# One time to landing for transfers of all sizes, in the planner that orders the instructions of an attention and mixer kernel

## The chip, the cores and the metric

The kernel runs on one core of a Trainium2 chip. The metric is device time in microseconds (us) of one execution. Five engines work from instruction streams of their own, each in order: PE (matmuls and transposes), ACT, DVE and POOL (elementwise work), and SP, which here issues every DMA.

## The reference, cut to what matters

All data are float32. Attention over 4 batches, 12 heads, 448 tokens, head size 64, with RMS-normalised q and k; then a gated block with a spatial matrix over the tokens; then a token mixer and a channel mixer with a residual.

```python
q_n, k_n = rmsnorm(q, g_q), rmsnorm(k, g_k)
attn = softmax(q_n @ k_n.T / 8);  x = attn @ v            # 48 heads, then (4, 448, 768)
h = relu(x @ w_in);  u, v = h[..., :512], h[..., 512:]    # w_in 768x1024
v_s = w_spatial @ layernorm(v) + b_spatial                # over the tokens
x = (u * v_s) @ w_out                                     # w_out 512x768
u = x + (relu(x.T @ w_tok1) @ w_tok2).T                   # 448 -> 256 -> 448
out = u + relu(u @ w_ch1) @ w_ch2                         # 768 -> 1536 -> 768
```

## The kernel before, in words

The work is recorded first and ordered afterwards. Every call on `nc` makes an `Op` with an engine, a cost, and a time `late` that passes after its end until its result can be seen elsewhere. `Plan.issue` (L365) then places all ops: a greedy list schedule (`place`, L263) runs over all engines at once, each engine taking, of the ops that are ready by the plan's own clock, the one with the least weight. It is run forward, the weights are taken from a run backward, and so on for eight rounds; the forward run with the shortest planned span is kept, and the ops are issued in its order of start times. So each engine's stream, SP's queue and the choice of PSUM banks all come from `estimate` (L214). What it returns never delays anything on the chip: there each engine takes its stream in order and waits on semaphores. An op that the plan holds ready and the chip does not, stops all that stands behind it on its engine.

For a transfer `estimate` gives two numbers (L244, L245): the time that SP is taken, the size over 260 bytes per ns and at least 475 ns, and the time to landing after that. `hop` (L257) adds `late` to the end of an op for whoever waits for it, SP itself included.

The stages are these.

- Attention, 24 pairs of heads. A pair's q and k come by six DMAs into a tile `raw` (two buffers): two `raw<-in_q`, then `raw<-in_k` in parts of 112x4x64, 64x64, 112x3x64 and 48x64. ACT squares them (`sq`), DVE sums (`ss`), POOL works out the root with two ACT calls `ry` and scales `raw` in place; PE transposes (`tp`), ACT evicts (`whole` for the first eight pairs, `qt` and `kt` later). Then scores `sc`, maxima `nm` on DVE, exponentials `e` on ACT with sums, transposes of `e` (`tp`), evictions `et`, products with v (`av`), results `xp`.
- Beside it the weights are prepared, float64 words turned to pairs of float32r: `word` and `wv` for w_in's second half (512 KB loads), `wpart` for all other weights in pieces (256 KB loads and two 128 KB stores to scratch each). ACT, DVE and POOL all take part.
- The gated block of a batch (`vps`, `ups`, `sps`, `xps`) can start when six pairs of the batch are done; the first three batches run beside the attention. It loads prepared weights (`wu` 768 KB, `wo` 1 MB) from scratch and stores `xo` to `x_d`.
- The last gated block runs beside the token mixer's start (`h1ps`, `u_ps`), then the channel mixer (`h2ps`, `o_ps`) runs to the end.

Of the kernel before, what the change touches and what calls it, by code (L numbers as in the profile page):

```python
# [149 lines left out]
class Plan:  # L150
# [63 lines left out]
    def estimate(self, engine, fn, out, ins, kwargs):  # L214

        shape = max((tuple(x.shape) for x in [out] + ins if isinstance(x, Part)), key=free)
        n = free(shape)
        psum = any(x.tile.psum for x in ins)
        if engine == "tensor":
            if fn == "transpose":  # L220
                return ins[0].shape[0] / 1.2 + 3, 200
            n = free(ins[1].shape)
            if ins[1].dtype == F32R:
                return 0.326 * n if ins[0].shape[0] <= 64 else n / 2.4 + 13, 200
            if ins[0].shape[0] <= 64:
                return 1.04 * n, 200
            return n / 1.2 + 54 if out.shape[0] <= 64 else n / 0.6, 200
        if engine == "scalar":
            extra = any(isinstance(kwargs.get(k), Part) for k in ("bias", "scale"))
            extra += kwargs.get("accum_out") is not None  # L230
            return 0.833 * n + (51 if psum else 94) + 93 * extra, 142
        if engine == "vector":
            if n <= 64:
                return 160, 128
            if fn in ("tensor_scalar", "tensor_copy") and not psum:
                return 0.53 * n + 90, 128
            pointer = fn == "scalar_tensor_tensor" and any(free(x.shape) == 1 for x in ins)
            return 1.042 * n + 70 + 61 * pointer, 175 if free(out.shape) < n else 128
        if engine == "gpsimd":
            if fn == "tensor_scalar":  # L240
                return max(165, 1.3 * n + 35), 75
            pace = 2.0 if any(x.steps and x.steps[-1][0] == "to_broadcast" for x in ins) else 2.4
            return max(165, pace * n + 20), 75
        size = shape[0] * n * 4  # L244
        return max(475, size / 260), 2400 + 1.2e-3 * size  # L245

    def fence(self, pools, act):

# [173 lines left out]
def free(shape):  # L422
    n = 1
    for x in shape[1:]:
        n *= x
    return n
# [905 lines left out]
```

## Time and profile before

| | |
|---|---|
| median of 3 runs | 947.33 us (947.18 to 949.82) |
| the profiled execution | 946.97 us |
| its span | 944.7 us |
| PE busy | 912.2 us (97%) |
| weight loads (PEld) busy | 738.3 us (78%) |
| DVE, ACT, POOL busy | 574.9, 454.1, 342.9 us |

PE is TensorE's matmuls, and a transpose counts as a matmul; DMA issue is not counted as busy. Rows name a group as output<-input. Source lines of the recorded ops are all that of the helper that issues them (L406), so one goes by tile names. Busy shares are averages over stages with different limits: attention alone at the start, gated blocks and attention mixed, then matmuls alone.

### The profile page before, as it was taken

To read this page: it belongs to the slowest core of one execution; us is meant where nothing else is said; L and a number is where in the kernel's file an instruction comes from. 1 tells how busy PE (TensorE), PEld (TensorE's weight loads), DVE (VectorE), ACT (ScalarE), POOL (GpSimd) and SP (SyncE) were. 2 spreads that over 40 slices of the span, in tenths; PEclk is the share of its full clock that TensorE was granted. 3 is DMA by queue.
4 is the path that set the end of the run, shared out by engine and by line. 5 is a ranking of instruction groups with operands and counts; after the bars stand their busy time and mean duration, and the time that the engine had idled before them with its cause. 6 is when DMAs were issued, how large, how long until landed. Compare 5 with 4: busy or idle time off the path is not lost.

```text
span 944.7 us, 15517 instructions
## 1 busy us (share of the span) xinstructions
PE 912.2 (97%) x5368; PEld 738.3 (78%) x5368; DVE 574.9 (61%) x1234; ACT 454.1 (48%) x1145; POOL 342.9 (36%) x478
## 2 busy tenths in 40 slices
PE   3888999999999999999999999999999999999998
PEld 1444465777767776677899999899899999999898
DVE  3988888765886767853151367635655546565434
ACT  4998978776686766764342344311312212122100
POOL 3565454784667744565044023100201102011100
PEclk9999999999999999999999999999999999999999
DMA  6555655457445465222764384721211112111024
GB/s 168 145 132 155 172 154 157 134 166 202 115 110 162 143 195 170 76 79 98 244 196 156 119 277 156 272 75 34 84 51 50 52 34 83 51 51 51 17 87 147
DMA packets 124653, 118.57 MB, mean 126 GB/s; under 512 B 74784, under 2 KB 108128, under 8 KB 123040
## 3 DMA queue, kind: packets, MB, share of 16 engines
q1 hardware_dynamic: 124576, 117.59, 41.3%
q8 instruction: 42, 0.69, 0.3%
q14 instruction: 35, 0.29, 0.1%
HBM read 89.77 MB, written 27.79 MB: 124 GB/s over the span
## 4 chain that ended last, share of the span: by engine, by line
PE 81%; ACT 8%; DMA 4%; DVE 2%; SPq 1%; issue 1%; POOL 1%; ACTq 0%; POOLq 0%
PE o_ps L406 19%; PE h2ps L406 18%; PE tp L406 8%; PE av L406 6%; PE xps L406 6%; PE vps L406 5%; PE sc L406 5%; PE ups L406 5%; PE sps L406 4%; ACT e L406 3%; PE u_ps L406 3%; PE h1ps L406 3%; SPq L406 1%; ACT et L406 1%; DMA x_d<-xo 1%
## 5 line engine op out<-in xcount | busy, mean ns | idle before, releaser
L406 PE MATMUL o_ps<-c,h 128*128 128x384 f32 x1008 | 179.9, 337 | 0.0
L406 PE MATMUL h2ps<-ut,c 128*128 128x512 f32 (+1 forms) x864 | 179.4, 364 | 0.0
L406 PEld LDWEIGHTS o_ps<-c,h 128*128 128x128 f32 x1008 | 175.0, 188 | 2.1 <-DVE acc L406 0.5
L406 PEld LDWEIGHTS h2ps<-ut,c 128*128 128x128 f32 x864 | 148.0, 189 | 24.1
L406 POOL TENSOR_TENSOR c<-word,c 128x384 fp32r<-128x384 f32 x40 | 40.5, 1014 | 271.8 <-ACT c L406 252.2
L406 ACT ACTIVATE e<-sc,nm 112x448 f32<-112x448 f32 x192 | 120.9, 639 | 31.6 <-PE tp L406 16.9
L406 DVE TENSOR_REDUCE nm<-sc 112x1 f32<-112x448 f32 x192 | 110.4, 615 | 25.1 <-PE sc L406 24.9
L406 PE MATMUL tp<-ident,e 112*128 112x112 f32 x672 | 96.7, 263 | 3.7 <-ACT et L406 1.3
L406 PEld LDWEIGHTS tp<-ident,e 112*128 112x128 f32 x672 | 73.5, 140 | 32.6 <-ACT et L406 7.4
L406 DVE TENSOR_TENSOR acc<-o_ps,acc 128x384 f32<-128x384 f32 x140 | 77.4, 556 | 29.5 <-PE o_ps L406 28.9
L406 POOL TENSOR_SCALAR e<-e,sums 112x448 f32<-112x448 f32 x112 | 71.2, 652 | 35.8 <-DVE sums L406 9.0
L406 ACT ACTIVATE c<-word 128x384 fp32r<-128x384 f32 x40 | 21.0, 525 | 128.3 <-DVE word L406 63.6
L406 ACT ACTIVATE h<-h2ps 128x512 fp32r<-128x512 f32 (+1 forms) x48 | 25.9, 539 | 111.7 <-PE h2ps L406 111.4
L406 DVE SCALAR_TENSOR_TENSOR h<-h2ps,h 128x512 fp32r<-128x512 f32 (+1 forms) x48 | 30.0, 624 | 80.8 <-ACT h L406 80.7
L406 ACT ACTIVATE et<-tp 128x448 f32<-128x448 f32 x120 | 65.1, 551 | 16.2 <-PE tp L406 13.8
L406 PE MATMUL ups<-xp,wu 128*128 128x448 f32 x288 | 69.9, 378 | 0.0
L406 PE MATMUL av<-et,v 128*64 128x448 f32 x288 | 66.7, 559 | 0.8 <-ACT et L406 0.5
L406 PE MATMUL xps<-wo,g 128*128 128x256 f32 x432 | 62.7, 291 | 0.4 <-ACT xo L406 0.4
L406 PEld LDWEIGHTS xps<-wo,g 128*128 128x128 f32 x432 | 54.9, 190 | 5.1 <-issue 2.0
L406 PEld LDWEIGHTS ups<-xp,wu 128*128 128x128 f32 x288 | 51.7, 188 | 6.8 <-ACT e L406 1.4
L406 DVE TENSOR_SCALAR word<-word 128x384 f32<-128x384 f32 (+1 forms) x92 | 35.1, 382 | 35.8 <-ACT word L406 34.3
L406 PE MATMUL vps<-wv,xp 128*128 128x512 f32 x216 | 56.0, 403 | 0.0
(112 smaller groups left out, 1460.0 us busy)
## 6 DMA issues: line engine op xcount, KB each, us to landing
raw<-in_moe_w_ch_dram SPq DMA_DIRECT2D x40, 384.0 KB, 3.2
wu<-wu_d SPq DMA_DIRECT2D x16, 768.0 KB, 4.7
wo<-wo_d SPq DMA_DIRECT2D x12, 1024.0 KB, 5.0
raw<-in_q_dram SPq DMA_DIRECT2D x48, 112.0 KB, 2.7
acc<-u_d SPq DMA_DIRECT2D x14, 384.0 KB, 8.2
out_dram<-o SPq DMA_DIRECT2D x28, 192.0 KB, 1.9
v<-in_v_dram SPq DMA_DIRECT2D x48, 96.0 KB, 2.6
x_d<-xo SPq DMA_DIRECT2D x36, 128.0 KB, 2.4
```

The costliest lines, as they stand in the source:

```text
L406: getattr(getattr(self.nc, op.engine), fn)(*args, **kwargs)
```

## The change

`estimate` returned for a transfer a landing time of 2400 ns plus 1.2 ns for every 1000 bytes; it returns 2000 ns for every size. The time that SP is taken stays as it was.

```diff
@@ -241,8 +241,7 @@
                 return max(165, 1.3 * n + 35), 75
             pace = 2.0 if any(x.steps and x.steps[-1][0] == "to_broadcast" for x in ins) else 2.4
             return max(165, pace * n + 20), 75
-        size = shape[0] * n * 4
-        return max(475, size / 260), 2400 + 1.2e-3 * size
+        return max(475, shape[0] * n * 4 / 260), 2000
```

No instruction is added or removed. The plan is another one on all engines, since a small shift of one start time moves all later choices; in the channel mixer the two orders are the same but for the last blocks. The file is one line shorter, so the same helper is L405 in the rows after.

SP's queue where the first two pairs have been asked for; `v_221` and `v_154` are the v tile of pair 0 under two numbers. Before:

```order
L406 DMA g<-in_g_k_dram 64x1
L406 DMA raw<-in_moe_w_in_dram 128x1024 x3
L406 DMA raw<-in_q_dram 112x4x64 x2
L406 DMA raw<-in_k_dram 112x4x64
L406 DMA raw<-in_k_dram 64x64
L406 DMA raw<-in_k_dram 112x3x64
L406 DMA raw<-in_k_dram 48x64
L406 DMA raw<-in_moe_w_in_dram 128x2x256
L406 DMA v_221<-in_v_dram 128x3x64 x2
```

The same place of SP's queue now:

```order
L405 DMA g<-in_g_k_dram 64x1
L405 DMA raw<-in_moe_w_in_dram 128x1024 x2
L405 DMA v_154<-in_v_dram 128x3x64 x2
L405 DMA vrest<-in_v_dram 64x64
L405 DMA raw<-in_q_dram 112x4x64 x2
L405 DMA raw<-in_k_dram 112x4x64
L405 DMA raw<-in_k_dram 64x64
L405 DMA raw<-in_k_dram 48x64
L405 DMA raw<-in_k_dram 112x3x64
L405 DMA vrest<-in_v_dram 64x64
L405 DMA raw<-in_moe_w_in_dram 128x1024
```

Pair 0's v stands ahead of pair 2's q and k, the third 512 KB load of w_in behind them, and the larger of a pair's last two k parts comes last instead of last but one (it does so for nearly all pairs).

ACT's stream at the same time, where pair 0's transposes are evicted (`whole`) and pair 1's root is begun (`ry`); `raw_128` is the first 512 KB of w_in. Before:

```order
L406 ACTIVATE sq_149<-raw_113 112x512
L406 ACTIVATE word_164<-raw_128 128x512
L406 ACTIVATE whole_169<-tp_154 128x448
L406 ACTIVATE whole_172<-tp_162,gg_144 128x448
L406 ACTIVATE ry_177<-ra_159 112x16
L406 ACTIVATE ry_177<-ry_177 112x16
```

And now:

```order
L405 ACTIVATE sq_149<-raw_113 112x512
L405 ACTIVATE word_152<-raw_128 128x512
L405 ACTIVATE ry_167<-ra_161 112x16
L405 ACTIVATE whole_172<-tp_156 128x448
L405 ACTIVATE whole_177<-tp_165,gg_143 128x448
L405 ACTIVATE ry_167<-ry_167 112x16
```

The first `ry` of pair 1 has moved ahead of pair 0's evictions; `word` still stands ahead of all of them.

SP's queue in the second gated block, where `xo` goes to `x_d` and a later pair's q and k are asked for. Before:

```order
L406 DMA x_d_67<-xo 128x256 x3
L406 DMA raw<-in_q_dram 112x4x64 x2
L406 DMA raw<-in_k_dram 112x4x64
L406 DMA wo<-wo_d_65 128x2048
L406 DMA x_d_66<-xo 64x256
L406 DMA x_d_67<-xo 64x256
L406 DMA raw<-in_k_dram 64x64
```

And now:

```order
L405 DMA x_d_67<-xo 128x256 x2
L405 DMA wo<-wo_d_65 128x2048
L405 DMA x_d_66<-xo 64x256
L405 DMA x_d_67<-xo 64x256
L405 DMA raw<-in_q_dram 112x4x64 x2
L405 DMA raw<-in_k_dram 112x4x64
L405 DMA x_d_67<-xo 128x256
L405 DMA raw<-in_k_dram 64x64
```

The two small stores of `xo` stand ahead of the pair's loads instead of among them.

## Rows read from the trace of the kernel before

**Rows 1.** The page: the span, and each engine's busy time.
```profile
span 944.7 us, 15517 instructions
PE 912.2 (97%) x5368; PEld 738.3 (78%) x5368; DVE 574.9 (61%) x1234; ACT 454.1 (48%) x1145; POOL 342.9 (36%) x478
```

**Rows 2.** Busy time by stretch: from:to length, engines with counts, PEclk, DMA share, GB/s.
```profile
core 0: us, PE busy (x) PEld busy (x) DVE busy (x) ACT busy (x) POOL busy (x), PEclk, DMA share, GB/s
0.00:25.00 25.00, 8.81 (x32) 4.01 (x32) 10.80 (x21) 13.09 (x30) 8.67 (x21) 1.00 0.64 160
25.00:116.70 91.70, 81.29 (x489) 40.64 (x489) 78.45 (x174) 84.59 (x235) 53.90 (x76) 1.00 0.55 154
116.70:460.00 343.30, 341.32 (x2179) 246.20 (x2178) 236.73 (x548) 237.21 (x645) 199.77 (x309) 1.00 0.49 142
460.00:930.00 470.00, 469.56 (x2607) 436.59 (x2605) 242.91 (x482) 118.87 (x236) 80.55 (x72) 1.00 0.33 105
930.00:944.70 14.70, 11.20 (x70) 10.88 (x68) 6.00 (x11) 0.38 (x1) 0.00 (x0) 1.00 0.41 148
```

**Rows 3.** Waits of PE, 0 to 130 us: total us, times, longest.
```profile
PE sc L406 <- ACT e L406: 4.0, 6, 1.1
```

**Rows 4.** Timeline of ACT, 9 to 17.5 us: start, us, instruction, idle before it.
```profile
14.91 0.66 ACT L406 ACTIVATE word<-raw 128x512 f32<-128x512 f32 x1 [2.03 <-DMA raw<-in_moe_w_in_dram]
15.47 0.54 ACT L406 ACTIVATE whole<-tp 128x448 f32<-128x448 f32 x1
16.42 0.22 ACT L406 ACTIVATE ry<-ra 112x16 f32<-112x16 f32 x1
```

**Rows 5.** Timeline of PE, 10 to 24 us.
```profile
10.86 1.75 PE L406 MATMUL tp<-ident,raw 112*128 112x112 f32 x8 [10.86 <-POOL raw L406]
16.59 5.00 PE L406 MATMUL sc<-whole 64*112 64x448 f32 x12 [3.97 <-ACT whole L406]
```

**Rows 6.** Timeline of SP, 9 to 14 us.
```profile
9.68 1.53 SPq L406 DMA_DIRECT2D raw<-in_moe_w_in_dram  x3
12.78 1.05 SPq L406 DMA_DIRECT2D raw<-in_q_dram  x2
```

**Rows 7.** Timeline of POOL, 12 to 22 us.
```profile
20.56 1.26 POOL L406 TENSOR_TENSOR wv<-word,wv 128x512 fp32r<-128x512 f32 x1
```

**Rows 8.** ACT's groups, 0 to 116.7 us: count, busy us, mean ns, idle before.
```profile
L406 ACT ACTIVATE e<-sc,nm 112x448 f32<-112x448 f32 x60 | 37.9, 642 | 6.1 <-PE tp L406 4.5 <-DVE nm L406 1.5
L406 ACT ACTIVATE sq<-raw 112x512 f32<-112x512 f32 x20 | 12.8, 642 | 6.8 <-DMA raw<-in_q_dram 3.7 <-DVE ss L406 2.2 <-DMA raw<-in_k_dram 0.9
L406 ACT ACTIVATION_READ_ACCUMULATOR e<-sc,nm 112x1 f32 x60 | 12.8, 213 | 0.0
L406 ACT ACTIVATE wpart<-raw 128x256 f32<-128x256 f32 x12 | 5.5, 457 | 0.3 <-DMA wu_d<-wpart 0.3
```

**Rows 9.** DMA issues, 0 to 120 us: count, KB each, median us to landing.
```profile
raw<-in_moe_w_in_dram SPq DMA_DIRECT2D x6, 512.0 KB, 5.3
raw<-in_moe_w_in_dram SPq DMA_DIRECT2D x12, 256.0 KB, 3.0
raw<-in_q_dram SPq DMA_DIRECT2D x22, 112.0 KB, 2.6
raw<-in_k_dram SPq DMA_DIRECT2D x10, 84.0 KB, 2.3
raw<-in_k_dram SPq DMA_DIRECT2D x10, 12.0 KB, 2.0
```

**Rows 10.** DMA issues of the whole span.
```profile
acc<-u_d SPq DMA_DIRECT2D x14, 384.0 KB, 8.2
x<-x_d SPq DMA_DIRECT2D x12, 384.0 KB, 5.0
```

**Rows 11.** Timelines of PE and of ACT, 334 to 352 us.
```profile
347.56 0.39 ACT L406 ACTIVATE xo<-xps 128x256 f32<-128x256 f32 x1 [1.21 <-DMA x_d<-xo]
349.11 0.87 PE L406 MATMUL sc<-kt,qt 64*112 64x448 f32 x6 [0.50 <-ACT xo L406]
```

## The prediction, made before the changed kernel was run

> **What bounds the kernel now.** I read the page first: PE is busy for 912.2 of 944.7 us [rows 1], so the whole idle time of the engine that carries the work is 32.5 us. The table by stretch says where that idle time lies [rows 2]: 16.2 us of it before 25 us (25.00 less 8.81), 10.4 us from 25 to 116.7 us (91.70 less 81.29), 2.0 us from there to 460 us, 0.4 us up to 930 us and 3.5 us at the end. The granted clock is 1.00 in all of them, the upper level of 2.4 GHz, so no time goes to the clock. The reader is to see two regimes. Up to 116.7 us, where the first gated block's matmuls begin, only attention is there, and ACT is the fullest engine: 84.59 of 91.70 us, 92%. After it PE always has some other matmul to do, and ACT is busy for 237.21 of 343.30 us, 69%. An order can win or lose much only where PE has nothing else, before 116.7 us.
>
> Then I looked at what PE waits for at the start. It stands until 10.86 us for the first scaled pair, and again for 3.97 us, until 16.59 us, for ACT's eviction `whole` [rows 5]. ACT was late there because `word` stood ahead of it in its stream and waited for w_in's first 512 KB until 14.91 us [rows 4]. That is the pattern to look for in this change: an op placed ahead of work that was ready, whose load had not landed. PE's waits for ACT's exponentials come to another 4.0 us in the first 130 us [rows 3].
>
> **What the plan believes, before and after.** For a load the plan counts SP's time and then the landing; the trace gives the time from issue to landing.
>
> - 512 KB of w_in (524288 bytes): before 2.02 + 3.03 = 5.05 us, now 4.02; the trace says 5.3 [rows 9].
> - 256 KB (262144 bytes): before 3.72, now 3.01; the trace says 3.0 [rows 9].
> - a pair's q, 112 KB (114688 bytes): before 0.475 + 2.538 = 3.01, now 2.475; the trace says 2.6 [rows 9].
> - 384 KB of x (393216 bytes): before 4.38, now 3.51; the trace says 5.0, and 8.2 for the same size where fourteen `acc` loads go together [rows 10].
>
> So the old numbers held a reserve of 0.4 to 0.7 us for the small and middle sizes and were short for the loads that meet others; the new ones are about right for the small and middle sizes, without reserve, and shorter still for the large ones.
>
> The Trainium skill, "DMA: Bandwidth & Descriptors", section "Anatomy of one DMA", gives a fixed part of about 2.0 us that doesn't grow with the size, and a part per byte at 436 GB/s, which is the form that the changed line takes. By it 512 KB would take an estimated 3.2 us, less than even the new plan expects, and the term for lost reserve below would be nothing: the sum would come to 947.4 us. The trace does not agree for this size: 5.3 us [rows 9]. The sum goes by the rows.
>
> **The change part by part.** No instruction comes or goes, so every term is one of place.
>
> 1. Start, SP. The larger of the last two k parts now comes last. It takes 2.3 us to land where the smaller takes 2.0 [rows 9], so pair 0's k is complete some 0.3 us later and PE's first transposes begin at about 11.1 us. They then end well before 14.91 us, when `word` lets ACT go on [rows 4, 5], so this is hidden: 0. Without that cover it costs 0.3.
> 2. Start, SP again. Three transfers of v move ahead of pair 2's q and k. SP has nothing to issue from 11.21 us (9.68 + 1.53) to 12.78 us, since pair 2 needs the buffer that pair 0's transposes free [rows 5, 6]. Three issues at about 0.5 us each (three took 1.53) fill that hole: 0. The third load of w_in, which paid for it, was asked for at about 10.7 us and was used only after both pairs were scored; it stays early enough by several us, since it is issued behind pair 2's loads, some 17 us in.
> 3. Start, ACT. One `ry` of 0.22 us now stands between `word` and pair 0's evictions [rows 4], on the path to the first scores: +0.2.
> 4. Start, POOL. The order puts the 1.26 us `wv` ahead of the scaling of pair 1 [rows 7]; in the same place PE now does pair 0's last two score matmuls ahead of pair 1's transposes, in place of waiting. I take 0; without that cover it costs 1.3.
> 5. To the first gated block. The block needs the sixth `xp` on ACT. By the two orders ACT has 60 `e` in place of 59, 22 `wpart` in place of 21 and 18 `sq` in place of 19 ahead of it, all else equal: 0.642 + 0.213 + 0.457 - 0.642 = +0.67 us [rows 8]. ACT is at 92% there, so it counts: +0.7.
> 6. Lost reserve. From 25 to 116.7 us ACT takes the squares of six more pairs, each behind a q load that the plan now has landed 0.125 us too early: 6 x 0.125 = +0.8 (rounded up, since medians hide the later half). Bounds: nothing, if everything is asked for long before; and 5 x 1.3 = 6.4 us, if the five 512 KB conversions after the first each stand for what the plan is short, 5.3 - 4.02. I take the value near nothing because `raw` has two buffers, so a pair is asked for almost a pair ahead.
> 7. The second gated block. The small `x_d` stores now go ahead of a pair's loads. Before, ACT stood for such a store and PE for ACT, 0.50 us [rows 11]: -0.5 if that goes; what is late next there is the transpose of the next pair, which PE replaces by other matmuls.
> 8. The rest of the mixed stretch: PE's idle time is 2.0 us in all [rows 2], so a better order wins at most that, and a worse one first uses up the other matmuls: 0, bounds -2 and +3.
> 9. From 460 us on: the orders of the channel mixer agree but for its last blocks, and PE idles 0.4 us before 930 us: 0. The changes of PE between its full and its half-array forms (scores and v products on one side) are 170 in both orders, so nothing is added there.
>
> Sum: 0.2 + 0.7 + 0.8 - 0.5 = +1.2 us on the profiled execution's 946.97 us, which is 0.36 below the median of the runs: 948.2 us, or 0.1% over the median of 947.33. 0.3% is 2.8 us, about what a measurement can tell from no change: from 944.5 to 950.2 us the result counts as the same.
>
> **Rivals.**
>
> *Slower: ACT stands in front of loads.* The mechanism of the start (`word` waiting 2.03 us, [rows 4]) comes back at the conversions up to 116.7 us, because the plan thinks 512 KB to be there 1.3 us sooner than it is. For it: the new plan cuts exactly the part that was already short, and ACT has only 7.1 us of slack in 91.7 [rows 2]. Against it: in the new order the third 512 KB load is issued some 9 us ahead of its use, and in the old plan, short by 0.25 us, only the first of the six conversions waited. Price: terms 3 and 5 with 6.4 in place of 0.8, less the 0.5: 946.97 + 0.2 + 0.7 + 6.4 - 0.5 = 953.8 us. It decides once conversions stand for more than about 0.6 us each.
>
> *Faster: reserve was idle time.* The old plan held ops back for data that had landed 0.4 to 0.7 us earlier, and PE idles 10.4 us in the attention stretch [rows 2]. If the plan with the truer small sizes closes four tenths of that, -4.2, the time is 946.97 + 0.2 + 0.7 - 0.5 - 4.2 = 943.2 us. For it: most transfers of that stretch are of the sizes for which 2000 ns is nearly right. Against it: ACT is at 92%, and its work is the same; PE's named waits are for ACT, not for transfers [rows 3].
>
> *Not faster and not slower, but by a trade in the token mixer.* x loads take 5.0 us and are planned at 3.51 [rows 10]. If four batches' first matmuls each stood 1.5 us, it would be 948.2 + 6 = 954.2 us. Against it: the order has x asked for a batch ahead, and PE idles 0.4 us there now.
>
> **How the numbers follow.** Forecast (no change that can be measured) 0.45. Slower through ACT 0.25, through the token mixer 0.05. Faster through the reserve 0.25. A reshuffled order on every engine has many small terms of either sign that I can't list, and the first two rivals both start from the stretch in which PE has no cover. Faster by over 0.3%: 0.25; within: 0.45; slower: 0.30. The range goes from the middle of the faster case (943.2) to just beyond the slower one: 943.0 to 954.0 us. The forecast's own range is 944.5 to 950.2.
>
> **What would show it.** PE's first transposes at about 11.1 us and first scores at about 16.8 us (terms 1, 3); v landed by 14 us; the first `vps` matmul between 116 and 119 us (terms 5, 6); ACT's idle time before `word`, `wpart` and `sq` for DMA no more than 2 us over before's in the first 116 us; PE's wait at the second block's `xo` gone; PE idle at most 3 us from 116.7 to 460 us; the channel mixer the same length to 0.5 us. I'm wrong if the first `vps` moves by more than 3 us, or if PE idles where it had cover.

## The result, and the profile after

The changed kernel takes 959.17 us (median of 4 runs, 957.76 to 960.3) against 947.28 us before (4 runs beside it, 947.18 to 949.82): 1.0111 times, 95% interval 1.0096 to 1.0125 (this ratio is worked out from all the runs; the quotient of the two medians is 1.0126). The forecast was 948.2, the range ended at 954.0. The profiled execution has a span of 958.3 us, 13.6 more than before, and the same matmuls.

The page of the changed kernel, its span and busy times, answers to [rows 1]:

```profile
span 958.3 us, 15497 instructions
PE 915.9 (96%) x5368; PEld 740.7 (77%) x5368; DVE 559.1 (58%) x1234; ACT 455.6 (48%) x1145; POOL 344.2 (36%) x478
```

PE is busy 3.7 us longer for as many matmuls and idles 42.4 us (958.3 less 915.9) in place of 32.5. These two, 3.7 and 9.9, are the whole 13.6 us.

Busy time by stretch answers to [rows 2]. The first cut is again the first `vps`, the second lies at the same place in the work as 460 us did before (the token mixer's first `h1ps` starts 12.0 us later, at 493.7 in place of 481.7 us, so 472):

```profile
core 0: us, PE busy (x) PEld busy (x) DVE busy (x) ACT busy (x) POOL busy (x), PEclk, DMA share, GB/s
0.00:25.00 25.00, 8.21 (x32) 4.00 (x32) 11.38 (x22) 12.73 (x30) 8.88 (x21) 1.00 0.65 159
25.00:124.20 99.20, 85.20 (x489) 42.30 (x489) 80.30 (x178) 85.85 (x236) 54.73 (x77) 0.95 0.53 147
124.20:472.00 347.80, 341.33 (x2186) 247.60 (x2185) 221.07 (x544) 238.48 (x647) 203.01 (x309) 1.00 0.48 139
472.00:943.60 471.60, 469.98 (x2601) 435.88 (x2601) 239.82 (x481) 118.15 (x234) 77.59 (x72) 1.00 0.32 104
```

The reader is to see three losses. Up to the first gated block 7.5 us: the same 489 matmuls, as many of each shape, need 85.20 us where they needed 81.29, at a granted clock of 0.95 in place of 1.00, which is 3.9 us, and PE idles 14.0 us in place of 10.4, which is the other 3.6. In the mixed stretch 4.5 us (347.80 against 343.30): PE idles 6.5 us where it idled 2.0. And 1.6 us behind it (471.60 against 470.00), of which idle time is 1.2. PE waits there (472 to 943.6 us) in the last gated block and in the token mixer, and nowhere in the channel mixer:

```profile
PE h1ps L405 <- ACT xh L405: 0.9, 1, 0.9
PE vps L405 <- ACT xo L405: 0.6, 1, 0.6
```

So the loss is spread over three stretches, and no single wait makes it.

The start came as forecast. ACT (timeline, 9 to 17.5 us) answers to [rows 4]:

```profile
15.06 0.66 ACT L405 ACTIVATE word<-raw 128x512 f32<-128x512 f32 x1 [2.27 <-DMA raw<-in_moe_w_in_dram]
15.63 0.20 ACT L405 ACTIVATE ry<-ra 112x16 f32<-112x16 f32 x1
15.73 0.53 ACT L405 ACTIVATE whole<-tp 128x448 f32<-128x448 f32 x1
```

PE (timeline, 10 to 24 us) answers to [rows 5]:

```profile
10.94 1.75 PE L405 MATMUL tp<-ident,raw 112*128 112x112 f32 x8 [10.94 <-POOL raw L405]
16.84 4.53 PE L405 MATMUL sc<-whole 64*112 64x448 f32 x12 [4.15 <-ACT whole L405]
```

From there on PE's waits (0 to 130 us: total, times, longest) grow; the first of them answers to [rows 3]:

```profile
PE sc L405 <- ACT e L405: 5.1, 5, 2.3
PE tp L405 <- POOL wide L405: 2.1, 2, 1.9
PE tp L405 <- ACT e L405: 2.0, 2, 1.2
```

The landing times (0 to 120 us: count, KB each, median us) answer to [rows 9]; the second last line, the stores of converted weights, is one that the prediction did not look at. It was 2.7 us before, for 22 of them:

```profile
raw<-in_moe_w_in_dram SPq DMA_DIRECT2D x6, 512.0 KB, 5.5
raw<-in_moe_w_in_dram SPq DMA_DIRECT2D x12, 256.0 KB, 3.4
wu_d<-wpart SPq DMA_DIRECT2D x22, 128.0 KB, 3.1
raw<-in_q_dram SPq DMA_DIRECT2D x20, 112.0 KB, 2.8
```

Every one of them is longer than before (5.3, 3.0, 2.7, 2.6). The plan of 2000 ns has the 256 KB at 3.01 us and the 128 KB store at 0.50 + 2.00 = 2.50: in its own order it is short by 0.4 and 0.6, where with the old order's landings it would have been exact for the one and short by 0.2 for the other. The old plan had 3.72 and 3.06 for them, and a reserve of 0.7 and 0.4. (The Trainium skill, "DMA: Bandwidth & Descriptors", "Anatomy of one DMA", fits a fixed 2.0 us and 436 GB/s to transfers that POOL issues, which gives an estimated 2.6 us for 256 KB. Here SP issues them all, which the prediction did not say, and the trace has 3.0 before and 3.4 after.)

### How far the chip runs behind the plan

`place` gives every instruction a time at which it is to start. The difference between that and the trace says where an order comes apart. Here for POOL's scaling of a pair (`raw<-raw,ry`, one for each of the 24 pairs), and at the end the span less the plan's own end. The last two rows are kernels of the experiments below:

```
us late at pair   1    2    4    6    7   10   16   22   24   end   plan's end
before         -1.1  2.2  3.1  2.3  2.3  2.7  4.2  4.1  6.0  10.0     934.7
changed, 2000  -0.6  3.2  5.7  4.7  8.3 10.1 11.9 15.8 15.8  24.1     934.2
2270           -0.7  0.6  1.1  1.1  1.5  0.9  1.5  3.0  3.2   9.8     935.4
3200           -2.0 -1.3  1.8  1.5  1.7  1.9  1.6  1.3  1.4   4.1     941.4
```

The changed plan promises 0.6 us less than the old one (before rounding) and falls 14 us further behind. Before, the chip is 2 to 5 us late from pair 2 to pair 22; after the change it loses ground all the way, with the largest step after pair 2 (3.6 us) between pairs 6 and 7, at 65 to 81 us. Read in the same way, the other orders made with one time of 2060 ns or less have pair 24 scaled 7.0 to 13.2 us late, and 2540 has it 5.8 us late. Each row is one execution, and a difference of 2 us in it says little: three executions with the same order up to there scaled pair 4 at 38.2, 38.9 and 40.6 us (e18, the changed kernel and e17).

### The profile page after: what moved, and what is told of

It reads as the page before. It is cut to its first block, busy times and chain, and to the rows that moved or that the text cites. A ratio compares the mean times of both kernels' runs of the same rounds, so it can differ in the third digit from the quotient of the medians.

```text
span 958.3 us, 15497 instructions
## 1 busy us (share of the span) xinstructions
PE 915.9 (96%) x5368; PEld 740.7 (77%) x5368; DVE 559.1 (58%) x1234; ACT 455.6 (48%) x1145; POOL 344.2 (36%) x478
## 3 DMA queue, kind: packets, MB, share of 16 engines
q1 hardware_dynamic: 124576, 117.59, 40.6%
## 4 chain that ended last, share of the span: by engine, by line
PE 80%; ACT 8%; DMA 4%; DVE 3%; POOL 2%; issue 2%; SPq 1%; ACTq 0%; POOLq 0%; DVEq 0%
PE o_ps L405 18%; PE h2ps L405 18%; PE tp L405 9%; PE vps L405 6%; PE av L405 6%; PE sc L405 5%; PE ups L405 5%; PE xps L405 5%; ACT e L405 4%; PE h1ps L405 3%; PE sps L405 3%; PE u_ps L405 3%; DMA x_d<-xo 1%; SPq L405 1%; ACT et L405 1%
## 5 line engine op out<-in xcount | busy, mean ns | idle before, releaser
L405 PE MATMUL o_ps<-c,h 128*128 128x384 f32 x1008 | 179.6, 337 | 0.0
L405 PE MATMUL h2ps<-ut,c 128*128 128x512 f32 (+1 forms) x864 | 179.1, 364 | 0.0
L405 PEld LDWEIGHTS o_ps<-c,h 128*128 128x128 f32 x1008 | 174.9, 188 | 2.0 <-DVE acc L405 0.5
L405 PEld LDWEIGHTS h2ps<-ut,c 128*128 128x128 f32 x864 | 148.2, 189 | 24.5
L405 ACT ACTIVATE e<-sc,nm 112x448 f32<-112x448 f32 x192 | 120.4, 636 | 33.2 <-DVE nm L405 23.1
L405 POOL TENSOR_TENSOR c<-word,c 128x384 fp32r<-128x384 f32 x40 | 40.5, 1014 | 265.0 <-ACT c L405 237.7
L405 DVE TENSOR_REDUCE nm<-sc 112x1 f32<-112x448 f32 x192 | 110.5, 615 | 30.1 <-PE sc L405 29.6
L405 PE MATMUL tp<-ident,e 112*128 112x112 f32 x672 | 98.5, 266 | 9.2 <-ACT e L405 3.6
L405 PEld LDWEIGHTS tp<-ident,e 112*128 112x128 f32 x672 | 75.1, 142 | 37.8 <-ACT et L405 10.2
L405 DVE TENSOR_TENSOR acc<-o_ps,acc 128x384 f32<-128x384 f32 x140 | 77.3, 555 | 29.5 <-PE o_ps L405 28.3
L405 POOL TENSOR_SCALAR e<-e,sums 112x448 f32<-112x448 f32 x112 | 76.2, 700 | 34.4 <-DVE sums L405 12.1
L405 ACT ACTIVATE h<-h2ps 128x512 fp32r<-128x512 f32 (+1 forms) x48 | 25.9, 540 | 116.6 <-PE h2ps L405 114.9
L405 ACT ACTIVATE c<-word 128x384 fp32r<-128x384 f32 x40 | 21.0, 525 | 123.0 <-DVE word L405 58.2
L405 DVE SCALAR_TENSOR_TENSOR h<-h2ps,h 128x512 fp32r<-128x512 f32 (+1 forms) x48 | 30.0, 625 | 81.2 <-ACT h L405 81.2
L405 ACT ACTIVATE et<-tp 128x448 f32<-128x448 f32 x120 | 65.2, 550 | 15.8 <-PE tp L405 13.5
L405 PE MATMUL ups<-xp,wu 128*128 128x448 f32 x288 | 70.3, 379 | 0.0
L405 PE MATMUL av<-et,v 128*64 128x448 f32 x288 | 67.1, 564 | 0.1
L405 PE MATMUL xps<-wo,g 128*128 128x256 f32 x432 | 61.7, 290 | 0.9 <-ACT g L405 0.8
L405 PEld LDWEIGHTS xps<-wo,g 128*128 128x128 f32 x432 | 54.7, 190 | 6.6 <-issue 2.4
L405 PE MATMUL vps<-wv,xp 128*128 128x512 f32 x216 | 55.8, 403 | 0.6 <-ACT xo L405 0.6
L405 PEld LDWEIGHTS ups<-xp,wu 128*128 128x128 f32 x288 | 51.7, 189 | 5.4 <-issue 1.0
L405 DVE TENSOR_SCALAR word<-word 128x384 f32<-128x384 f32 (+1 forms) x92 | 33.7, 367 | 37.1 <-ACT word L405 35.1
```

The lines of the kernel that those rows point to most:

```text
L405: getattr(getattr(self.nc, op.engine), fn)(*args, **kwargs)
```

## The experiments

Sixteen kernels (e1 to e16) are the one before with another second value in `estimate`'s return for transfers, that is, another landing time and a new order made from it; e11 has a third buffer for `xo` besides. Each result stands with its ratio to the kernel before, which was run beside it (medians of 948.1 to 948.9 us), and the 95% interval of the ratio. Each diff below shows only the new line, which stands for:

```diff
-        return max(475, size / 260), 2400 + 1.2e-3 * size
```

### Is it the level, or would any reshuffled order do it?

One nanosecond more or less is no difference to the chip, but gives other orders. e1 and e2 are around the old formula, e3 and e4 around the new value.

```diff
+        return max(475, size / 260), 2401 + 1.2e-3 * size     # e1
+        return max(475, size / 260), 2399 + 1.2e-3 * size     # e2
+        return max(475, size / 260), 2001                     # e3
+        return max(475, size / 260), 1999                     # e4
```

> The old rule with 2401 ns in place of 2400, which changes nothing in what the plan knows but moves most of PE's order. Theory 'reserve' (the flat 2000 ns is slower because it takes away the reserve, and any order made with the old rule is good): within 3 us of before, 944 to 951 us. Rival 'lottery' (any reshuffle moves the time by several us, and the order before was a lucky one): anywhere from 945 to 960 us, more likely 950 to 957.

> The old rule with 2399 ns, which changes only about a tenth of PE's order. Both theories: close to before where the orders agree; 'reserve' 945 to 950 us, 'lottery' 945 to 955 us.

> 2001 ns for all sizes, an order unlike that of 2000. 'Reserve': 955 to 962 us, like the change. 'Lottery': anywhere from 945 to 960 us, most likely 948 to 956, and not the same as with 2000.

> 1999 ns for all sizes. As for 2001: 'reserve' 955 to 962 us; 'lottery' 945 to 960 us, and another time than with 2000 and 2001.

Measured: e1 946.33 us (0.9969 times before, 0.9957 to 0.9981), e2 949.01 (0.9996, 0.9985 to 1.0008), e3 955.26 (1.0066, 1.0037 to 1.0094), e4 959.16 (1.0096, 1.0067 to 1.0126). The orders of e1 and e3 are really other ones: PE's differ from their neighbour's from the 45th and the 65th of 5112 matmuls on. That any reshuffle costs 12 us is out. But e3 is 4 us better than the change with the same level, and two are weak witnesses: PE's order in e4 is that of the change for its first 1265 matmuls, in e2 that of before for the first 1667.

### One time for all sizes, or too short a time?

```diff
+        return max(475, size / 260), 2000 if size < 120000 else 2400 + 1.2e-3 * size            # e5
+        return max(475, size / 260), 2000 if 120000 < size < 270000 else 2400 + 1.2e-3 * size   # e6
+        return max(475, size / 260), 2000 if size > 270000 else 2400 + 1.2e-3 * size            # e7
+        return max(475, size / 260), 2540                                                       # e8
```

> 2000 ns only for transfers under 120000 bytes (the parts of q, k and v), the old rule for the rest. 'Reserve of the attention loads' (the pairs' q and k arrive late and ACT stands): 954 to 960 us. 'Reserve of the prepared weights' or 'of the large loads': 945 to 950 us.

> 2000 ns only for 120000 to 270000 bytes (the 256 KB loads and 128 KB stores of the prepared weights, the 128 KB stores of xo), the old rule for the rest. 'Reserve of the prepared weights' (wpart waits for a load or a store on ACT): 954 to 960 us; the other two theories: 945 to 950 us.

> 2000 ns only above 270000 bytes (512 KB of w_in, wu, wo, x, acc, the channel weights), the old rule for the rest. 'Large loads' (my rival, ACT in front of loads that land 5 us after their issue): 953 to 960 us; the other two: 945 to 950 us.

> One time for all sizes, but 2540 ns, what the old rule gave for a pair's q. If the level is what counts: 945 to 951 us. If the dependence on the size is what counts: 953 to 960 us.

Measured: e5 948.55 (0.9996, 0.9979 to 1.0013), e6 952.18 (1.005, 1.0014 to 1.0086), e7 949.27 (1.0004, 0.9984 to 1.0023), e8 947.5 (0.9996, 0.9981 to 1.0011). That the time no longer depends on the size costs nothing (e8). Neither do short times for the large loads (e7), on which the prediction's slower rival rested, nor for the small ones. Only in e6 do the short times cost something by themselves, those of the middle sizes, loads of 256 KB ahead of a conversion and stores of 128 KB behind it: 0.5%, less than half of the change's 1.1%, and less than the 954 to 960 us that its theory expected. It is one order, so how much of its 0.5% belongs to the sizes and how much to that order is not shown.

### Loads or stores of the middle sizes, and more reserve

```diff
+        return max(475, size / 260), 2557 if size == 131072 else 2000                               # e9
+        return max(475, size / 260), 2400 + 1.2e-3 * size if 131072 < size < 270000 else 2000       # e10
+        return max(475, size / 260), 3200                                                           # e12
```

and e11, at 2000, with a ring of three `xo` tiles:

```diff
+        return max(475, size / 260), 2000
-                xo = mp.tile([P, NX], F32, tag="xo", bufs=2, name="xo")
+                xo = mp.tile([P, NX], F32, tag="xo", bufs=3, name="xo")
```

> 2000 ns for every transfer, but 2557 (what the formula of before gives) for the stores of 128 KB (wpart and xo). Theory "the stores' landing is short" (rings of two tiles: ACT waits on the landing of the store of two tiles ago; by the waits of the profiles 4.2 us before, 12.5 us in the changed kernel): most of the 12 us come back, 946 to 951. Theory "the loads of 256 KB are short" (planned 3.0 us, landing 3.0): little comes back, 954 to 960. If both are needed: 951 to 955.

> 2000 ns for every transfer, but the formula of before for those between 131072 and 270000 bytes without 131072 itself (loads of 256 KB ahead of a conversion, a few of 192 to 224 KB, the last stores of 192 KB). Theory "stores": still slow, 954 to 960. Theory "loads": 946 to 951. Both needed: 951 to 955.

> 2000 ns for every transfer, and a ring of three xo tiles in place of two, so that an xo never waits for the store of two ago (in the changed kernel ACT's waits of this kind add up to 3.6 us, two of them). Theory "the waits on the landing of stores are the cost": 2 to 4 us less than the changed kernel, 954 to 957, and the loss between 324 and 418 us smaller. Theory "the cost sits in the loads and in PE's cover, not in this wait": 958 to 961.

> One time for all sizes again, of 3200 ns: more reserve than before everywhere but on transfers of over 670 KB. Theory "reserve is what counts, and enough is enough": 945 to 950, no change against before. Theory "reserve is paid for in work that stands too early": 950 to 956.

Measured: e9 949.3 (1.0009, 0.999 to 1.0028), e10 949.27 (1.0012, 0.9997 to 1.0027), e11 950.08 (1.0007, 0.9988 to 1.0026), e12 948.47 (1.0003, 0.9983 to 1.0023). Both halves of the reserve brought nearly all of it back, each alone. e9 lies where "stores" had it and e10 where "loads" had it, so together they fit neither, and the middle expectation (951 to 955) is missed as well. e11 missed both of its ranges: it got back 9 us where the wait it removes was worth 3.6. Its order is a new one throughout (PE's from the 43rd matmul on), so this says more about the change's own order than about `xo`; and it is an order made with 2000 ns whose loss can't be told from none. And 3200 ns, too much for nearly everything, loses nothing.

The idea behind e9 and e11 came from ACT's waits for the landing of a store before it may write that buffer again (0 to 460 us). Before:

```profile
ACT wpart L406 <- DMA wo_d<-wpart: 2.4, 1, 2.4
ACT xo L406 <- DMA x_d<-xo: 1.2, 1, 1.2
ACT wpart L406 <- DMA w_d<-wpart: 0.3, 1, 0.3
ACT wpart L406 <- DMA wu_d<-wpart: 0.3, 1, 0.3
```

After:

```profile
ACT wpart L405 <- DMA c_d<-wpart: 3.9, 4, 1.6
ACT xo L405 <- DMA x_d<-xo: 3.6, 2, 2.0
ACT wpart L405 <- DMA wu_d<-wpart: 2.4, 2, 1.3
ACT wpart L405 <- DMA w_d<-wpart: 1.4, 2, 1.0
ACT wpart L405 <- DMA wo_d<-wpart: 1.2, 1, 1.2
```

4.2 us became 12.5, nearly the size of the loss. But the next table's 2270, as quick as before, has them too:

```profile
ACT xo L406 <- DMA x_d<-xo: 3.9, 3, 1.8
ACT wpart L406 <- DMA wo_d<-wpart: 3.5, 2, 1.8
ACT wpart L406 <- DMA c_d<-wpart: 3.1, 2, 1.7
```

With 0.4 us for w_d's 10.9 us of such waits, and no loss: what ACT waits is no measure of what PE loses. I gave the theory of the stores up.

### The level, drawn out

```diff
+        return max(475, size / 260), 1500     # e13; e14 1940, e15 2060, e16 2270
```

> One time of 1500 ns for all sizes: 0.5 us less than in the changed kernel, so that even the 128 KB stores (landing 2.4 to 2.7 us) and the q loads (2.6) are planned 0.5 to 0.7 us too short. Theory (a), the cost grows with what is missing: 962 to 975, slower than the changed kernel. Theory (b), it belongs to some plans: 947 to 960, anywhere.

> One time of 1940 ns: as good as the changed kernel's 2000, but a plan of its own. Theory (a): 956 to 962. Theory (b): 947 to 955, unlike the changed kernel.

> One time of 2060 ns: as good as the changed kernel's 2000, but a plan of its own. Theory (a): 953 to 959. Theory (b): 947 to 953, unlike the changed kernel.

> One time of 2270 ns, half way between 2000 and 2540. Theory (a): 950 to 954, half of the loss. Theory (b): 946 to 951, no loss.

All kernels with one time for all sizes and two `xo` buffers together (plan's end as above; the last column is the median less the plan's end, some 2 us of which lie around the span):

```
ns      median   ratio to before (interval)     plan's end   behind
1500    954.07   1.0070 (1.0049 to 1.0091)        932.5       21.6
1940    952.93   1.0050 (1.0033 to 1.0067)        934.4       18.5
1999    959.16   1.0096 (1.0067 to 1.0126)        934.2       25.0
2000    959.17   1.0111 (1.0096 to 1.0125)        934.2       25.0
2001    955.26   1.0066 (1.0037 to 1.0094)        935.0       20.3
2060    951.17   1.0022 (1.0007 to 1.0037)        933.6       17.6
2270    947.23   0.9985 (0.9971 to 0.9999)        935.4       11.8
2540    947.50   0.9996 (0.9981 to 1.0011)        935.6       11.9
3200    948.47   1.0003 (0.9983 to 1.0023)        941.4        7.1
```

Two things are to be seen. From 2270 up the time is that of before, and from 2060 down every interval lies above 1: the level counts, and it does so somewhere between 2060 and 2270. Below that there is no slope: 1500 is not the slowest. Theory (a) missed all four of its ranges and theory (b) met all four of its own. But (b) by itself gives no reason why all six orders from 2060 down are slower and none from 2270 up is, so the two go together: a level below which orders lose, and a loss that belongs to each order. Below it the plans scatter over 8 us, and the change is the worst of them. And what a plan promises says nothing: 1500 promises 8.9 us less than 3200 and takes 5.6 us more.

Busy time and granted clock of PE from 25 to 475 us, for 2270:

```profile
25.00:125.00 100.00, 89.30 (x532) 0.99 0.58 157
125.00:325.00 200.00, 198.75 (x1257) 1.00 0.51 142
325.00:475.00 150.00, 149.04 (x965) 1.00 0.51 154
```

for the changed kernel:

```profile
25.00:125.00 100.00, 86.00 (x494) 0.95 0.52 146
125.00:325.00 200.00, 196.75 (x1239) 1.00 0.52 146
325.00:475.00 150.00, 146.17 (x964) 1.00 0.44 135
```

2270 leaves PE idle for 10.7, 1.3 and 1.0 us, as the one before does (10.4, 1.1, 0.9); the changed kernel for 14.0, 3.3 and 3.8.

### Two places of the changed order by themselves

At 81 us the trace of the changed kernel has a pile-up. DVE (timeline, 78 to 105 us):

```profile
81.67 1.56 DVE L405 TENSOR_SCALAR sums<-sums 112x8 f32<-112x8 f32 x1 [1.42 <-ACT e L405]
```

POOL:

```profile
81.30 1.90 POOL L405 TENSOR_TENSOR raw<-raw,ry 112x1024 f32<-112x1024 f32 x1
84.02 0.61 POOL L405 COPY wide<-sums 112x512 f32<-112x512 f32 x1 [0.82 <-DVE sums L405]
```

PE:

```profile
84.68 0.60 PE L405 MATMUL tp<-ident,wide 112*128 112x112 f32 x4 [1.93 <-POOL wide L405]
...
85.98 1.84 PE L405 MATMUL sc<-whole 64*112 64x448 f32 x4 [0.24 <-ACT e L405]
```

and PE's clock (busy time, count, granted clock):

```profile
85.00:90.00 5.00, 4.75 (x23) 0.55 0.03 6
```

`sums`, 0.17 us elsewhere, ends 0.03 us after POOL's `raw` does; PE stands 1.93 us for `wide`, and then runs near the lower level: four score matmuls that take 1.01 us at full clock take 1.84. (The Trainium skill, "SBUF — State Buffer", "Who interferes with whom", says that POOL shares a pair of ports with DVE, that a DVE instruction which uses this pair, as a tensor_scalar can, contends with POOL for it, and that the one that comes second waits for the whole of the other's instruction; these rows agree, with 1.56 us in place of 0.17.) The plan had `raw` at 73.0 and `sums` at 76.4 us, well apart: it does keep such instructions apart, but only by its own clock, and here `raw` is 8.3 us late and `sums` 5.3.

e17 moves that `raw` behind `xp` and nothing else; e18 also moves ACT's `wpart` that waits 1.19 us for a store's landing at 69.07 us, which makes two neighbours on DVE change places. In the order of the change the numbers are those of the instructions:

```diff
         start = best[1]
+        start[653] = start[628] + 1         # e17, e18: raw behind xp, on POOL
+        start[559] = start[477] + 1         # e18 alone: wpart behind xp, on ACT
+        for i in sorted(range(len(ops)), key=lambda i: (start[i], i)):
+            start[i] = max([start[i]] + [start[d] + 0.001 for d in prev[i]])
```

> The order of the changed kernel, with one instruction moved: POOL's scaling of raw that starts at 81.30 us there goes behind wide and xp. Theory "the collision and the clock after it": DVE's sums take 0.2 us in place of 1.56, PE stands 0.5 us or less in place of 1.93 ahead of wide's transposes, and the clock stays at 1.00 from 85 to 92, which gives back 1.4 + 3.2 us: 953.5 to 956. Rival "PE stands too little to matter, the clock falls anyway": 957 to 958.5. Rival "slack ahead, given back later": 959 to 960, with first vps earlier and the end not.

> As e17, and a second instruction moved: ACT's wpart<-raw that waits 1.19 us at 69.07 for a store's landing goes three instructions later, behind the two exps and xp's copy. Theory "each such wait in front of ACT is paid in full": 1.0 to 1.2 us less than e17, 952.5 to 955. Rival "the wait is hidden, or given back by the next": as e17.

Measured: e17 956.86 (1.0088, 1.0053 to 1.0122), e18 958.13 (1.0089, 1.0065 to 1.0112). e17's DVE:

```profile
83.05 0.17 DVE L408 TENSOR_SCALAR sums<-sums 112x8 f32<-112x8 f32 x1 [1.42 <-ACT e L408]
```

its PE:

```profile
84.89 0.60 PE L408 MATMUL tp<-ident,wide 112*128 112x112 f32 x4 [0.76 <-POOL wide L408]
...
86.30 1.01 PE L408 MATMUL sc<-whole 64*112 64x448 f32 x4 [0.42 <-ACT e L408]
...
93.32 0.60 PE L408 MATMUL tp<-ident,e 112*128 112x112 f32 x4 [0.93 <-ACT whole L408]
```

and its clock there:

```profile
85.00:90.00 5.00, 4.24 (x32) 1.00 0.21 54
90.00:95.00 5.00, 3.91 (x26) 1.00 0.32 94
```

The collision is gone as expected, PE's wait is down to 0.76 us (0.5 or less was expected), and the clock stayed up in this execution. But PE now idles behind it, 0.76 us from 85 to 90 and 1.09 from 90 to 95 (5.00 less 4.24 and 3.91), and of the 4.6 us that were to come back the medians show 2.3 (956.86, between the ranges of the theory and of its first rival), which the intervals don't tell from none. The collision is real; that the loss hangs on it is not shown.

e18's ACT no longer waits for the store:

```profile
68.58 0.57 ACT L409 ACTIVATE xp<-over 128x448 fp32r<-128x448 f32 x1
69.05 0.42 ACT L409 ACTIVATE wpart<-raw 128x256 f32<-128x256 f32 x1
```

It is ahead of e17 by 2.0 us at `wide`'s transposes (82.9 against 84.9 us). But that is no gain of the move: it was ahead by 2.4 us already at POOL's scaling of pair 4, before the place where the two orders part. e17, then e18:

```profile
40.63 1.90 POOL L408 TENSOR_TENSOR raw<-raw,ry 112x1024 f32<-112x1024 f32 x1
38.23 1.90 POOL L409 TENSOR_TENSOR raw<-raw,ry 112x1024 f32<-112x1024 f32 x1
```

At the first `vps` it is 0.9 us behind e17 (123.6 against 122.7), with PE's clock lower on the way:

```profile
95.00:125.00 30.00, 25.47 (x135) 0.89 0.54 150
```

The time is as e17's, as the rival had it; whether the wait was hidden or given back these two executions don't tell.

## Why the prediction was wrong

**Terms 1 to 5, the start and ACT's added work: right, or nearly.** First transposes at 10.94 us (11.1 forecast), first scores at 16.84 (16.8), `ry` between `word` and `whole`. PE idles 0.6 us more before 25 us than before, where these terms had 0.2. Term 5 came out too: ACT is busy 98.6 us up to the first `vps` in place of 97.7, 0.9 us more where 0.7 was forecast.

**Term 6, the lost reserve: the step that failed.** It was +0.8 us, for squares that wait for q loads, with the 512 KB conversions as upper bound. Neither wait came: from 25 us to the first `vps` the traces show ACT waiting for no load at all, before or after the change. What it waits for there is the landing of 128 KB stores of converted weights, 2.4 us in place of 0.3 (the two rows `wu_d<-wpart` of ACT's waits above). The term looked at loads and left these stores out, 22 of them up to 120 us, behind each of which a buffer of a ring of two waits; their planned 2.50 us are 0.6 short in the new order. The prediction had also taken the landings of the old order for those of the new one, where they are 0.2 to 0.4 us longer. Its sign that ACT's waits for transfers grow by at most 2 us came out at 2.2 (9.1 against 6.9 us).

With term 5 this part was to come to +1.5 us; it came to 7.5. Of this, 3.9 us are longer busy time of PE at the lower clock, which the prediction did not price at all, because the clock was 1.00 throughout in the execution that it read. The other 3.6 us are idle time of PE. ACT's waits for stores and the stand behind `sums` are part of what is new there, but how much of the 3.6 us hangs on either is not shown.

**Terms 7 and 8, the mixed stretch: wrong.** The forecast was -0.5 and 0, bounds -2 and +3, because PE has other matmuls there. The stretch grew by 4.5 us. The wait at an `xo` that was to go came back larger at another place, on ACT:

```profile
357.68 0.39 ACT L405 ACTIVATE xo<-xps 128x256 f32<-128x256 f32 x1 [1.98 <-DMA x_d<-xo]
```

and on PE, where it was 0.50 us before [rows 11]:

```profile
358.12 0.32 PE L405 MATMUL tp<-ident,e 112*128 112x112 f32 x1 [1.54 <-ACT xo L405]
```

Cover in a list schedule is other work that stands at that place in the engine's own order. PE had work, but not next in its stream.

**Term 9, from 460 us on:** 0 forecast, 1.6 measured. It argued from the channel mixer, whose orders agree and where PE loses nothing, and left out the last gated block and the token mixer in the same stretch, whose orders differ: there PE waits 0.6 and 0.9 us.

**The rivals.** The slower one named the right direction and a time of 953.8, but the wrong mechanism: `word` waits for a 512 KB load only once up to there (2.27 us, 2.03 before), and short times for large loads alone cost nothing (e7). The faster one, "reserve was idle time", is refuted most plainly: 1500 ns has the least reserve and the earliest plan, and is 0.7% slower. The text had the point that decides: it said that I would be wrong if the first `vps` moved by more than 3 us or PE idled where it had cover. Both came.

**What is shown and what is not.** Shown: one time for all sizes is harmless (2270, 2540 and 3200 ns), and the level counts: with two `xo` buffers all six orders made with 2060 ns or less are slower, and none made with 2270 ns or more, or with the old formula, is. How the change's 12 us divide is not shown: four other orders below the level lose 2 to 7 us (1500, 1940, 2001 and 2060, by their ratios), e11 at 2000 ns with a third `xo` buffer nothing that can be told from none, which suggests that much of the 12 us is the change's own order. Argued only: that the middle sizes are part of it (e6). Not settled: why giving back either half of the middle sizes' reserve gives nearly all of it back, and which of the many small waits make up the loss; the two that I took out by themselves were worth 1 to 2 us together (1.0 by the medians, 2.1 by the ratios), and by the intervals perhaps nothing.

## What to carry to other kernels

A latency in a planner is not an estimate whose error should be zero on average. Here an order made with times near the median landing fell further behind its plan nearly all the way, and never caught up; that it does so at each transfer that is late is my reading and was not shown. Look at stores that free a buffer as well as loads, keep in mind that landing times differ from one order to the next, and when in doubt plan longer; here 2270 in place of 2000 ns cost nothing, and neither did 3200. Try any such constant at several values, with a nanosecond more and less beside each, before a difference of one per cent is put down to the constant.

## What the runs showed of the hardware that was not expected

- Landing times differ from order to order, one execution of each: 128 KB stores up to 120 us had a median of 3.1 us in the changed kernel, 2.7 before and at 1500 ns, 2.3 at 2270, and 2.2 at 3200 and in e11.
- A DVE instruction of 0.17 us took 1.56 us beside a 1.90 us POOL instruction, and ended with it.
- After PE had stood 1.93 us the granted clock was 0.55 from 85 to 90 us, near the lower of its two levels (1.2 of 2.4 GHz), and four score matmuls took 1.84 us in place of 1.01. In e17 it stayed at 1.00 behind a wait of 0.76 us.
- The mean clock goes with a part of the time, and is no trait of the kernel alone. Of 102 executions of the kernel before beside e1 to e18, the 27 with a mean clock of 0.999 or more took 947.7 us on average, the 20 with 0.995 or less 949.9. All four of the changed kernel had 0.995 or 0.996, so its loss of 12 us is far more than that. e17 had 1.00 at 957.08 us, 0.996 at 956.05 and 956.64, and 0.993 at 961.27.
